# Sketched attention and a leaky MLP in one kernel: v on every fourth partition, the first batch's features turned by TensorE, alpha turned later, a new order

## The chip, the cores and the metric

The kernel runs on one NeuronCore of a Trainium2 chip. The metric is the device time of one execution in microseconds (us), the median of several runs, lower is better. The core has TensorE (PE, matrix products; its weight loads are listed as PEld), VectorE (DVE), ScalarE (ACT), GpSimd (POOL) and SyncE (SP), whose queue issues nearly all the DMA transfers here. Products accumulate in PSUM, a memory of 8 banks; everything else lies in SBUF, 128 partitions wide.

## The reference, cut to what matters

There are 4 batches, 4 heads, 1,088 tokens, a head width of 32 and two sketches S1 and S2 of 8 rows each. The feature of a vector is the outer product of its two sketches, 64 numbers:

```python
phi(x) = (S1 x) outer (S2 x)                    # [.., 64]
kv  = sum over tokens of phi(k) v               # [64, 32] per batch and head
z   = sum over tokens of phi(k)                 # [64]
x   = (phi(q) kv) / (phi(q) z + 1e-6)           # attention output, [4352, 128] over batch and token
h   = x @ w_in                                  # [4352, 2048]
out = (max(h, 0) + alpha * min(h, 0)) @ w_out   # [4352, 128]
```

The kernel writes the leaky part as relu(h) times (1 - alpha) w_out plus x times a folded matrix W = w_in diag(alpha) w_out. W is computed once on the chip from bf16 high and low parts of w_out.

## The kernel before, in words

The kernel is a list of operations, each with its engine or engines, a cost in ns, dependences, buffers and a due time. A planner (`plan`) walks this list with a model of each engine and fixes the order in which each engine gets its instructions. Due times are worked out backwards from the end and then moved by a table `SHIFT`, one entry per operation name. Each engine then works through its instructions in the planned order; the waits follow from the dependences. A DMA load costs the planner 60 ns on the queue that issues it, and the table `FIRST` says when its data are taken to arrive, wherever the load stands in the queue.

*Loads.* SP issues k of batch 0 in two pieces (k0.0, k0.1), the first part of q (q0.0), v of batch 0 in four transfers (v0), the rest of q (q0.1), then the weights in halves (w_in0, w_out0, w_in1, w_out1), then k1, q1, v1. Batches 2 and 3 are loaded after the first stores. ACT's queue issues the sketches (`rows`), a small rest of k and alpha (`arows`). A partition holds 34 tokens of one head, and each head has 32 partitions. v is held with 32 neighbouring partitions for each quarter of the slots.

*Keys (`key_part`, `keys`).* k is turned by DVE (L592) in blocks of 32 x 32. PE makes the sketches (L598, operations "ab"), 32 rows at a time; DVE turns them back token-major (L601, "abT"). DVE or POOL form the outer products kp (L614). PE sums z (L638, L644) and kv (L653, L658, "kv0.0", "kv0.1", "kv1.0" and so on); z goes through a mask and a product with S1sel (L667, L670, "zM") and is added up by DVE into the third part of Wq (L673, "zW"), with which q's features give the denominator. kv is copied (bs), turned by PE (L681, "fin") and copied into kvW.

*Queries (`query_part`).* q is turned by DVE (L693). PE computes the features, two sketches and the denominator's weights in one go, 32 rows at a time (L699, "f"); it needs zW. DVE turns them (L705, "fT0" and "fT1"), multiplies (L711, "denm"), sums and inverts (L716, L717), scales (L721, "rec") and forms the outer product (L732, "ph"), then turns that (L735, "phT"). PE multiplies with kvW (L746, "num"); ACT or DVE copy the result as xT in bf16. Batch 0 is done in two parts, q0.0 and q0.1.

*Weights.* w_in is cast to bf16 (L362 on ACT, L364 on DVE) and turned by PE (L564, "winT"); w_out gives three bf16 versions (w_a, w_hi, w_lo: L548, L539, L362, L364), and PE forms W (L573).

*MLP (`mlp`).* For each group of tokens and each of 16 chunks of 128 hidden units, PE computes h (L812), ACT or DVE the relu (L818, L820), and PE adds the second product (L833, L830 in the last group). The first of them is called h0.0. DVE turns the result (L840), and SP stores it (L852).

While PE waits early on, it runs dummy matmuls on constants (L480); the planner fills gaps with one dummy per `DUMMY` ns until `FILL`. A load is entered like this:

```python
o = op("sp" if eng == "sp" else "act", 60, emit, due=-1e6 + len(ops), name="ld " + name)
o.arrive = t
```

Of the kernel before, what the change touches and what calls it, by code (L numbers as in the profile page):

```python
# [11 lines left out]
F32 = mybir.dt.float32  # L12
# [22 lines left out]
class Op:  # L35
# [24 lines left out]
FILL, DUMMY = 20000, 220.0  # L60
# [5 lines left out]
    "S": -162063, "S1rep": -165092, "S1sel": -117129, "Sq": -118882, "W": -37412, "W0": -22866, "W1": 15478,  # L66
    "W2": -15123, "W3": 1781, "W4": 2619, "W5": 51587, "W6": 25967, "W7": 192714, "W8": 115002, "W9": 219619,
    "Wmm": -33330, "alpha": -190724, "alphaT": -266286, "fin0": -14043, "fin1": 12778, "fin2": 12779, "fin3": 56137,
    "h0.0": -78145, "h0.1": -75522, "h0.10": -65056, "h0.11": -64907, "h0.12": -60138, "h0.13": -56202,
    "h0.14": -54167, "h0.15": -52572, "h0.2": -74191, "h0.3": -73871, "h0.4": -73366, "h0.5": -73505, "h0.6": -74028,  # L70
    "h0.7": -71518, "h0.8": -69689, "h0.9": -65371, "h1.0": -34789, "h1.1": -34107, "h1.10": -26669, "h1.11": -25965,
    "h1.12": -24240, "h1.13": -23831, "h1.14": -22996, "h1.15": -21303, "h1.2": -32211, "h1.3": -30635,
    "h1.4": -29890, "h1.5": -29256, "h1.6": -28989, "h1.7": -28705, "h1.8": -27953, "h1.9": -28414, "h2.0": -22166,
    "h2.1": -20590, "h2.10": -18021, "h2.11": -17163, "h2.12": -16727, "h2.13": -16702, "h2.14": -12616,
    "h2.15": -11871, "h2.2": -21026, "h2.3": -21311, "h2.4": -19650, "h2.5": -19181, "h2.6": -18910, "h2.7": -19344,
    "h2.8": -17740, "h2.9": -18101, "h3.0": -3542, "h3.1": -3314, "h3.10": -5050, "h3.11": -4032, "h3.12": -4085,
    "h3.13": -3612, "h3.14": -3253, "h3.15": -185, "h3.2": -3701, "h3.3": -4173, "h3.4": -4620, "h3.5": -4847,
    "h3.6": -4746, "h3.7": -4882, "h3.8": -5316, "h3.9": -4570, "h4.0": 1358, "h4.1": 1685, "h4.10": 1468,
    "h4.11": 1195, "h4.12": 1628, "h4.13": 2054, "h4.14": 1887, "h4.15": 2269, "h4.2": 1790, "h4.3": 2027,
    "h4.4": 1529, "h4.5": 1001, "h4.6": 2156, "h4.7": 2376, "h4.8": 2356, "h4.9": 2026, "h5.0": 623, "h5.1": 112,  # L80
    "h5.10": 629, "h5.11": 320, "h5.12": 6246, "h5.13": 6167, "h5.14": 5978, "h5.15": 5769, "h5.2": 1403, "h5.3": 942,
    "h5.4": 617, "h5.5": 311, "h5.6": -87, "h5.7": 177, "h5.8": 596, "h5.9": 1190, "h6.0": 6190, "h6.1": 6591,
    "h6.10": 13032, "h6.11": 16054, "h6.12": 17584, "h6.13": 21801, "h6.14": 21493, "h6.15": 24820, "h6.2": 6396,
    "h6.3": 6161, "h6.4": 5844, "h6.5": 5396, "h6.6": 5964, "h6.7": 9398, "h6.8": 11454, "h6.9": 12503, "h7.0": 24810,
    "h7.1": 25740, "h7.10": 39860, "h7.11": 39788, "h7.12": 40696, "h7.13": 42107, "h7.14": 48471, "h7.15": 65935,
    "h7.2": 31811, "h7.3": 31675, "h7.4": 34383, "h7.5": 34600, "h7.6": 36091, "h7.7": 36311, "h7.8": 37161,
    "h7.9": 37561, "h8.0": 65178, "h8.1": 67716, "h8.10": 91782, "h8.11": 93060, "h8.12": 93208, "h8.13": 95018,
    "h8.14": 105798, "h8.15": 109119, "h8.2": 67942, "h8.3": 67800, "h8.4": 70787, "h8.5": 81498, "h8.6": 82124,
    "h8.7": 84958, "h8.8": 87782, "h8.9": 90633, "h9.0": 115646, "h9.1": 118850, "h9.10": 171489, "h9.11": 175089,
    "h9.12": 186470, "h9.13": 195972, "h9.14": 195962, "h9.15": 220234, "h9.2": 130914, "h9.3": 130993,  # L90
    "h9.4": 132808, "h9.5": 137804, "h9.6": 144756, "h9.7": 145191, "h9.8": 147495, "h9.9": 158749, "ident": -173975,
    "identb": -65399, "k0.0T": -269499, "k0.0ab": -208500, "k0.0abT": -181386, "k0.0kp0": -186006, "k0.0kp1": -49805,
    "k0.1T": -226397, "k0.1ab": -204602, "k0.1abT": -147845, "k0.1kp0": -80610, "k0.1kp1": -126124, "k1T": -151807,
    "k1ab": -65617, "k1abT": -64202, "k1kp0": -53416, "k1kp1": -50262, "k2T": -49013, "k2ab": -24485, "k2abT": -23171,
    "k2kp0": -4748, "k2kp1": -20747, "k3T": 1061, "k3ab": -476, "k3abT": 976, "k3kp0": -5300, "k3kp1": 4934,
    "kv0.0": -128612, "kv0.1": -38075, "kv1.0": -12328, "kv2.0": -3408, "kv3.0": 3898, "kvW0": -45486, "kvW1": 1981,
    "kvW2": 13506, "kvW3": 1305, "kvc0": -39856, "kvc1": 5618, "kvc2": -187, "kvc3": 21281, "mask4": -7204,
    "masks": -230084, "o0.0": -68831, "o0.1": -35165, "o0.10": -11755, "o0.11": -37900, "o0.12": -22687,
    "o0.13": -2667, "o0.14": -19472, "o0.15": -17633, "o0.2": -26624, "o0.3": -50154, "o0.4": -53802, "o0.5": -52091,
    "o0.6": 7406, "o0.7": -19776, "o0.8": -55070, "o0.9": -22190, "o1.0": -19212, "o1.1": -10753, "o1.10": -12412,  # L100
    "o1.11": -9725, "o1.12": 12884, "o1.13": 5281, "o1.14": 5421, "o1.15": 10070, "o1.2": 5939, "o1.3": -7592,
    "o1.4": -1373, "o1.5": 16588, "o1.6": 16406, "o1.7": -12906, "o1.8": -12480, "o1.9": -13846, "o2.0": -13883,
    "o2.1": 7536, "o2.10": -3705, "o2.11": 12909, "o2.12": 5832, "o2.13": 6569, "o2.14": 7440, "o2.15": -481,
    "o2.2": 11555, "o2.3": -6618, "o2.4": 8785, "o2.5": 3950, "o2.6": -13616, "o2.7": -8748, "o2.8": 1638,
    "o2.9": -2544, "o3.0": -2366, "o3.1": 14406, "o3.10": 2060, "o3.11": 30488, "o3.12": 1602, "o3.13": 38819,
    "o3.14": -177, "o3.15": 4596, "o3.2": 406, "o3.3": 5117, "o3.4": 3644, "o3.5": 10266, "o3.6": 5165, "o3.7": 1159,
    "o3.8": 27826, "o3.9": 571, "o4.0": 2412, "o4.1": 11935, "o4.10": 29557, "o4.11": 4726, "o4.12": 19429,
    "o4.13": 19816, "o4.14": 19315, "o4.15": 10373, "o4.2": 4269, "o4.3": 8227, "o4.4": 42796, "o4.5": 32283,
    "o4.6": 17095, "o4.7": 24031, "o4.8": 6192, "o4.9": 30133, "o5.0": 14462, "o5.1": 22177, "o5.10": 17762,
    "o5.11": 14812, "o5.12": 36034, "o5.13": 93554, "o5.14": 18463, "o5.15": 89195, "o5.2": 58370, "o5.3": 17242,  # L110
    "o5.4": 63152, "o5.5": 13846, "o5.6": 58588, "o5.7": 14941, "o5.8": 24115, "o5.9": 52316, "o6.0": 24146,
    "o6.1": 55471, "o6.10": 45589, "o6.11": 53978, "o6.12": 28311, "o6.13": 24237, "o6.14": 36282, "o6.15": 26859,
    "o6.2": 108485, "o6.3": 118186, "o6.4": 118170, "o6.5": 24511, "o6.6": 76818, "o6.7": 185418, "o6.8": 65222,
    "o6.9": 53201, "o7.0": 53882, "o7.1": 159116, "o7.10": 70280, "o7.11": 85883, "o7.12": 81416, "o7.13": 219320,
    "o7.14": 125582, "o7.15": 145328, "o7.2": 220110, "o7.3": 219471, "o7.4": 87638, "o7.5": 86532, "o7.6": 271772,
    "o7.7": 97668, "o7.8": 52125, "o7.9": 218098, "o8.0": 95600, "o8.1": 100801, "o8.10": 188787, "o8.11": 126719,
    "o8.12": 191640, "o8.13": 206438, "o8.14": 130480, "o8.15": 139549, "o8.2": 114097, "o8.3": 159936,
    "o8.4": 194146, "o8.5": 132532, "o8.6": 188660, "o8.7": 119852, "o8.8": 118698, "o8.9": 126302, "o9.0": 155601,
    "o9.1": 265875, "o9.10": 251564, "o9.11": 247170, "o9.12": 207643, "o9.13": 239424, "o9.14": 211858,
    "o9.15": 265764, "o9.2": 198072, "o9.3": 216795, "o9.4": 176212, "o9.5": 162237, "o9.6": 188998, "o9.7": 188709,  # L120
    "o9.8": 220317, "o9.9": 255881, "oT0": -76595, "oT1": -13249, "oT2": -4976, "oT3": 3666, "oT4": 8797, "oT5": 9428,
    "oT6": 59626, "oT7": 86089, "oT8": 150669, "oT9.0": 181249, "oT9.1": 157151, "q0.0T": -206015, "q0.0den": -23594,
    "q0.0denm": -84715, "q0.0f": -154699, "q0.0fT0": -154405, "q0.0fT1": -84045, "q0.0num": -84185,
    "q0.0ph0": -127812, "q0.0phT0": -84287, "q0.0rec": -2266, "q0.0x0.0": -30236, "q0.0x0.1": -80540,
    "q0.1T": -127197, "q0.1den": -70835, "q0.1denm": -74338, "q0.1f": -127426, "q0.1fT0": -75331, "q0.1fT1": -93816,
    "q0.1num": -26548, "q0.1ph0": -45509, "q0.1phT0": -34568, "q0.1rec": -27567, "q0.1x1.0": -19689,
    "q0.1x1.1": -14970, "q1T": -78399, "q1den": -20535, "q1denm": -28588, "q1f": -27994, "q1fT0": 2661,
# [797 lines left out]
```

## Time and profile before

| what | value |
|---|---|
| median of 3 runs | 109.66 us (108.98 to 109.77) |
| profiled execution | 110.35 us, span 108.6 us |
| PE busy | 100.8 us (93%), 1,368 instructions |
| PEld, DVE, ACT, POOL busy | 51.7, 77.9, 69.7, 38.0 us |
| mean granted TensorE clock | 0.98 |
| DMA | 26,255 packets, 11.24 MB, mean 104 GB/s |

The span goes from the first to the last instruction on the core; the execution's own time is a little longer. The slices of the page are 40 equal parts of the span, each digit the busy share in tenths. PEclk is the granted TensorE clock in tenths of full speed. The chain of waits goes back from the last instruction: at each step to what released it, or to the instruction before it on its engine; each line there has a start, a length and what ran. In the table by stretches of time, the columns after the stretch are its length, busy us and number of instructions of PE, PEld, DVE, ACT and POOL, the granted clock, the share of 16 DMA engines and GB/s.

### The profile page before, as it was taken

How to read it: one execution, taken by the hardware profiler on the slowest of the kernel's cores; microseconds unless marked ns; L12 is line 12 of the kernel's file. 1: busy time of each engine (PE TensorE's matmuls, PEld its weight loads, DVE VectorE, ACT ScalarE, POOL GpSimd, SP SyncE). 2: the span in 40 equal slices, each digit the busy share in tenths (PEclk: the TensorE clock that was granted, in tenths of full speed). 3: DMA queues.
4: the chain of work that ended last, by engine and by line, in shares of the span. 5: the costliest groups of instructions: out<-in, count | busy, mean ns of one | idle time of the engine just before them, and what ended most of it. 6: DMA issues, size and time to landing. Idle time of an engine off the chain costs nothing.

```text
span 108.6 us, 3312 instructions
## 1 busy us (share of the span) xinstructions
PE 100.8 (93%) x1368; PEld 51.7 (48%) x1368; DVE 77.9 (72%) x139; ACT 69.7 (64%) x152; POOL 38.0 (35%) x28
## 2 busy tenths in 40 slices
PE   7949997999999999999999999999999999999930
PEld 2233454443556543533455444355444445788920
DVE  3256399999678899388399995895982677577710
ACT  0510534999622699299685976677895688788920
POOL 4007383059994650001946504908700000000000
PEclk9996799999999999999999999999999999999998
DMA  2999999700000037995990500050032023051221
GB/s 58 320 213 259 340 356 313 140 24 6 0 0 9 0 57 139 378 182 96 359 221 14 89 8 6 0 97 6 0 59 38 0 49 54 2 95 27 48 46 36
DMA packets 26255, 11.24 MB, mean 104 GB/s; under 512 B 17776, under 2 KB 25216, under 8 KB 26240
## 3 DMA queue, kind: packets, MB, share of 16 engines
q1 hardware_dynamic: 25840, 10.92, 40.9%
q8 instruction: 11, 0.18, 0.7%
q10 hardware_dynamic: 400, 0.11, 0.5%
q14 instruction: 4, 0.03, 0.1%
HBM read 8.80 MB, written 2.23 MB: 102 GB/s over the span
## 4 chain that ended last, share of the span: by engine, by line
PE 82%; DVE 7%; DMA 4%; ACTq 1%; issue 1%; ACT 0%
PE ps L812 28%; PE ps L833 28%; PE ps L746 5%; DMA arows<-in_moe_alpha_dram 4%; PE ps L480 4%; PE ps L653 3%; PE ps L573 2%; PE ps L699 2%; PE ps L598 2%; PE ps L830 2%; DVE ft__73 L705 1%; DVE tm__79 L711 1%; PE ps L638 1%; ACTq L384 1%; DVE pt__77 L735 1%; DVE ph__75 L732 1%
## 5 line engine op out<-in xcount | busy, mean ns | idle before, releaser
L812 PEld LDWEIGHTS <-w_in_bf 128*128 128x128 bf16 x160 | 15.2, 99 | 14.5 <-issue 2.3
L833 PEld LDWEIGHTS <-w 128*128 128x128 bf16 x144 | 13.7, 98 | 13.3 <-issue 2.2
L812 PE MATMUL ps<-xT__94,w_in_bf 128*128 128x512 bf16 (+1 forms) x80 | 20.0, 336 | 0.0
L812 PE MATMUL ps<-xT__93,w_in_bf 128*128 128x512 bf16 x64 | 19.3, 380 | 0.1
L818 ACT ACTIVATE rh__81<-ps 128x512 bf16<-128x512 f32 (+1 forms) x25 | 13.9, 556 | 4.9 <-PE ps L812 4.8
L614 POOL TENSOR_TENSOR kp__68<-ab__66 128x1152 f32<-128x1152 f32 (+1 forms) x4 | 8.1, 2022 | 24.0 <-DVE ab__66 L601 24.0
L480 PE MATMUL ps<-const-bfloat16-1.0 128*128 128x512 bf16 x33 | 12.2, 506 | 0.8 <-PEq L909 0.8
L818 ACT ACTIVATE rh__83<-ps 128x512 bf16<-128x512 f32 (+1 forms) x19 | 10.6, 557 | 1.5 <-PE ps L812 1.5
L818 ACT ACTIVATE rh__82<-ps 128x512 bf16<-128x512 f32 (+1 forms) x18 | 10.0, 555 | 1.3 <-PE ps L812 1.2
L732 POOL TENSOR_TENSOR ph__76<-ft__73 128x1024 f32<-128x1024 f32 (+1 forms) x3 | 8.6, 2856 | 4.8 <-DVE ft__73 L721 4.8
L818 ACT ACTIVATE rh__85<-ps 128x512 bf16<-128x512 f32 (+1 forms) x15 | 8.4, 562 | 2.0 <-PE ps L812 1.7
L833 PE MATMUL ps<-rh__81,w 128*128 128x512 bf16 (+1 forms) x24 | 8.6, 357 | 0.0
L818 ACT ACTIVATE rh__86<-ps 128x512 bf16<-128x512 f32 (+1 forms) x12 | 6.9, 571 | 2.6 <-PE ps L833 2.3
L833 PE MATMUL ps<-rh__82,w 128*128 128x512 bf16 (+1 forms) x21 | 7.6, 360 | 0.0
L746 PE MATMUL ps<-pt__77,kvW 32*32 32x288 f32 (+3 forms) x320 | 7.4, 353 | 0.1
L735 DVE STREAM_TRANSPOSE pt__77<-ph__75 128x1280 f32<-128x1280 f32 (+1 forms) x5 | 6.9, 1388 | 0.7 <-POOL ph__75 L732 0.7
L539 POOL TENSOR_TENSOR w<-w_out_f,w 128x512 bf16<-128x512 f32 x4 | 4.7, 1165 | 7.6 <-DVE w L364 5.5
L705 DVE STREAM_TRANSPOSE ft__73<-ps 128x576 f32<-128x576 f32 (+2 forms) x10 | 6.0, 638 | 1.7 <-PE ps L699 1.5
L614 POOL TENSOR_TENSOR kp__69<-ab__66 128x1152 f32<-128x1152 f32 x3 | 6.5, 2176 | 0.0
L833 PE MATMUL ps<-rh__83,w 128*128 128x512 bf16 (+1 forms) x18 | 6.5, 361 | 0.0
L833 PE MATMUL ps<-rh__84,w 128*128 128x512 bf16 (+1 forms) x18 | 6.4, 355 | 0.0
L833 PE MATMUL ps<-rh__85,w 128*128 128x512 bf16 (+1 forms) x18 | 6.4, 355 | 0.0
(144 smaller groups left out, 193.7 us busy)
## 6 DMA issues: line engine op xcount, KB each, us to landing
k<-in_k_dram SPq DMA_DIRECT2D x3, 544.0 KB, 4.2
q<-in_q_dram SPq DMA_DIRECT2D x3, 544.0 KB, 7.8
out_dram<-oT__89 SPq DMA_DIRECT2D x24, 64.0 KB, 1.9
v<-in_v_dram SPq DMA_DIRECT2D x9, 128.0 KB, 7.0
w_in_f<-in_moe_w_in_dram SPq DMA_DIRECT2D x2, 512.0 KB, 6.3
w_out_f<-in_moe_w_out_dram SPq DMA_DIRECT2D x2, 512.0 KB, 6.4
v<-in_v_dram SPq DMA_DIRECT2D x6, 144.0 KB, 7.5
k<-in_k_dram SPq DMA_DIRECT2D x2, 256.0 KB, 3.8
```

What stands on the lines that cost most here:

```text
L480: nc.tensor.matmul(PS[:, 7], ones(128), ones(512), start=True, stop=True, skip_group_check=True)
L539: return lambda e: (nc.vector if e == "dve" else nc.gpsimd).tensor_tensor(out=out, in0=a, in1=b, op=what)
L573: nc.tensor.matmul(ps(bw)[:, :3 * DM], winT[:, c], w3[:, c].rearrange("p y m -> p (y m)"), start=c == 0, stop=c == NC - 1)
L614: (nc.vector if e == "dve" else nc.gpsimd).tensor_tensor(out=dst, in0=i0, in1=i1, op=ALU.mult)
L653: nc.tensor.matmul(ps(bk)[32 * h:32 * h + 32, :R], v_sb[b][:, h, vs], at(sb(bkp[h // 2]), x, [[1, R]]), start=first and i == 0, stop=False ...
L705: nc.vector.transpose(at(sb(bf)[:, 0], 2 * y * D, [[D, 2], [H * D, ns], [1, D]]), ps(f2[y])[:, :, :n].rearrange("p h (s t) -> p h s t", t=D))
L732: (nc.vector if e == "dve" else nc.gpsimd).tensor_tensor(out=dst, in0=i0, in1=i1, op=ALU.mult)
L735: oT.append(op("dve", dv(k) + 35, lambda e, lo=lo, hi=hi, bph=bph: nc.vector.transpose(sb(bp)[:, lo:hi].rearrange("p a b -> p (a b)"), sb( ...
L746: nc.tensor.matmul(ps(n2[c // 2])[32 * h:32 * h + 32, c % 2, :w * D], kvW[b][P, y, h], at(sb(bp)[P, 0], (2 * h + y) * D, [[2 * H * D, w], ...
L812: nc.tensor.matmul(ps(b)[:, :n], w_in_bf[:, c * 128:(c + 1) * 128], xs(), start=True, stop=True)
L818: nc.scalar.activation(sb(br)[:, :n], ps(b)[:, :n], ACTF.Relu)
L833: nc.tensor.matmul(ps(bo)[:, :n], w, y(), start=c == 0, stop=c == NC)
```

## The change

- **v on every fourth partition.** Token slots are now dealt out so that quarter c of the slots lies on partitions c, c+4, c+8 and so on, 9 slots for the first three quarters and 7 for the last, padded with zeros by a DVE memset ("pads") on which all v loads now depend. k is turned into the same order by two DVE instructions, with zeros set by POOL ("pads2"). The remainders of z and kv over 32 or 64 rows go away.
- **Batch 0's features token-major from PE.** The weights of these products are 128 tokens of turned k or q, and the moving side is the small sketch matrix. The results come out token-major, so that a copy on ACT or DVE stands where DVE turned them. For q, the denominator's part is a product of its own ("w", from Ww0), 8 or 10 products each, and denm reads it from PSUM.
- **Alpha turned later.** Its turn on PE now depends on the product that replicates the sketches (S1rep). The rest of k is no longer on ACT's queue.
- **Order planned anew.** The planner's costs, `FIRST` and `SHIFT` are new (the entry of "pads" is 19620207), `DUMMY` is 320, w_in's cast and w_hi may run on POOL, denm and rec too, and the memset "zero" counts 1,700 ns.

The order that the planner now gives SP is k0.0, k0.1, q0.0, w_in0, w_out0, q0.1, w_in1, w_out1, k1, q1, v0, v1, and after them the first store. PE gets 7 dummies, the turn of the sketches, S1rep, the turn of alpha, k0.0ab, a dummy, k0.1ab, z0.0, a dummy, z0.1, q0.0f, zM0, kv0.0, q0.0w, kv0.1, winT0, fin0, 4 dummies, q0.1f, a dummy, q0.1w, num0.0, winT1 and then h0.0. DVE gets, after denm, sums, reciprocal and scaling of q0.0: w_a, the copy of winT0, the turn of q0.1, phT of q0.0. POOL gets ph of q0.0; both copies of the first x are ACT's. In the new file the line of h is L881, of kv L699, of batch 0's query products L748, of the outer product ph L802.

```diff
-FILL, DUMMY = 20000, 220.0
+FILL, DUMMY = 20000, 320.0
...
+    for o in reversed(ops):
+        for d in [] if o.late else o.deps:
+            d.due = min(d.due, o.due)
     waiting = sorted(ops, key=lambda o: o.due)
...
+    def pads(e):
+        for x in v_sb:
+            nc.vector.memset(x[:, :, 7:9], 0.0)
+
+    def pads2(e):
+        nc.gpsimd.memset(kZ[1], 0.0)
+        for x in tiles["kT"]:
+            nc.gpsimd.memset(x, 0.0)
+
+    c_pad = op("dve", 1, pads, due=-2e7, name="pads")
...
     def load_v(b):
         for c in range(4):
+            n = 9 if c < 3 else 7
+            load(f"v{b}", "sp", v_sb[b][c:128:4, :, :n].rearrange("p h s d -> p h (s d)"),
+                 bass.AP(tensor=v.tensor, offset=(b * H * S + 9 * c) * D, ap=[[NT * D, 32], [S * D, H], [1, n * D]]),
+                 32 * H * n * D * 4).deps.append(c_pad)
...
-    load_k0("k0.0", 0)
-    load_k0("k0.1", 1)
+    load_k0("k0.0", 0, 4)
+    load_k0("k0.1", 4, 5)
     load_rows("q0.0", q_sb, q, 0, 0, 16)
-    load_v0()
-    load_rows("q0.1", q_sb, q, 0, 16, NT)
+    load_v(0)
     load_w_in(0)
     load_w_out(0)
+    load_rows("q0.1", q_sb, q, 0, 16, NT)
...
-    op("dve", 1150, zeros, due=-1e7, name="zero")
+    op("dve", 1700, zeros, due=-1e7, name="zero")
...
     o = op("pe", 180, lambda e: nc.tensor.transpose(ps(b_al)[:, :NC], arows, ident[:NC, :NC]),
-           [c_id] + got("arows"), [b_al], 200, name="alphaT", mode=1, ni=2)
+           [c_id, c_rep] + got("arows"), [b_al], 200, name="alphaT", mode=1, ni=2)
...
+        def turned(e):
+            for s in range(ns):
+                for hp in range(2):
+                    P = slice(64 * hp, 64 * hp + 64)
+                    nc.tensor.matmul(ps(pair)[:, hp, s * D:s * D + D], kT()[P, 4 * D * s:4 * D * s + 4 * D],
+                                     Wk[P].rearrange("p a b c -> p (a b c)"), start=True, stop=True, skip_group_check=True)
...
+            def kv(e, bkp=bkp, base=base, ns=ns, lo=lo, first=first, last=last):
+                for s in range(ns):
                     for h in range(H):
                         x = (base[h // 2] + 2 * s + h % 2) * R
+                        nc.tensor.matmul(ps(bk)[32 * h:32 * h + 32, :R], v_sb[b][:, h, lo + s], at(sb(bkp[h // 2]), x, [[1, R]]),
+                                         start=first and s == 0, stop=last and s == ns - 1, skip_group_check=True)
...
+            def rows_of(w, wide, dst):
+                def f(e):
+                    for s in range(ns):
+                        for hp in range(2):
+                            P = slice(64 * hp, 64 * hp + 64)
+                            x = 4 * D * s if s < 4 else (nj - 4) * D
+                            nc.tensor.matmul(ps(dst)[:, hp, s * wide:s * wide + wide], sb(bT)[P, x:x + 4 * D], w(P), start=True, stop=True,
+                                             skip_group_check=True)
+                return f
...
+            ot.append(op("pe", 100 * ns + 60, rows_of(lambda P: Ww0[P], 2 * r, bw), [oq, w_done[b]], [bT, bw], 200,
+                         name=tag + "w", mode=1, ni=8 * ns))
...
+                nc.vector.tensor_mul(at(sb(bt)[:, 0], 0, [[24 * ns, 2], [12, 2 * ns], [1, r]]), at(sb(bf)[:, 0], r, [[2 * ns * D, 2], [D, 2 * ns], [1, r]]),
+                                     at(ps(bw), 0, [[512, 2], [r, 2 * ns], [1, r]]))
```

## The prediction

> **What bounds the kernel now.** I read the page's slices first: they show when TensorE (PE) is full.
>
> ```profile
> PE   7949997999999999999999999999999999999930
> PEclk9996799999999999999999999999999999999998
> DMA  2999999700000037995990500050032023051221
> ```
>
> A slice is 2.7 us. From the ninth (about 22 us) until near the end PE is at 9; before that it partly waits and runs dummy matmuls (L480), and the DMA engines are at 9 from the second slice into the seventh. So the time is a front until the first MLP matmul, a body that PE bounds, and a tail. The chain of waits, in order of time, gives the borders.
>
> ```profile
> 12.51 0.58 PE ps L653 x32
> ...
> 13.87 0.56 PE ps L699 x32
> ...
> 14.45 0.79 DVE ft__73 L705 x2
> ...
> 18.80 1.25 DVE pt__77 L735
> ...
> 21.80 0.37 DVE xT__93 L364
> ...
> 22.22 1.47 PE ps L812 x6
> ```
>
> The first L812 starts at 22.22, 8.35 us after q0.0's features (L699 at 13.87). The last L830 ends at 104.04. Front 22.2, body 81.8 (PE busy 81.8 in the stretches from 22.2 to 104.1: nothing to win there but PE work), tail 4.6: span 108.6. The profiled execution took 110.35, 1.75 beyond its span and 0.69 over the median of 109.66. I add the difference to both.
>
> Next, stretches of time: the two last columns are the DMA share and GB/s.
>
> ```profile
> 0.00:6.00 6.00, 4.42 (x10) 1.31 (x10) 1.74 (x8) 1.49 (x2) 1.22 (x8) 1.00 0.71 189
> 6.00:12.00 6.00, 5.18 (x53) 1.97 (x53) 3.30 (x7) 0.74 (x3) 3.03 (x2) 0.73 1.02 258
> 12.00:18.00 6.00, 5.45 (x145) 3.28 (x145) 5.25 (x12) 2.08 (x5) 3.31 (x3) 0.99 1.10 362
> 18.00:22.00 4.00, 3.89 (x114) 1.97 (x111) 3.86 (x8) 3.78 (x10) 0.00 (x0) 1.00 0.81 144
> ```
>
> The DMA engines are full from 2 to 18 us: what stands behind in SP's queue lands late. The weights show it. Issued at 6.40, 6.88, 7.50 and 9.95, they landed (issue plus time to landing) at 11.6, 13.3, 15.0 and 16.4: in order of issue, 1.6 us apart for 512 KB.
>
> **The change part by part.** The step that decides is a moved DMA. SP issued v0 fourth, behind k0's two pieces and q0.0, and kv0.0 (L653) ran at 12.51. Now SP issues k0, q0.0, w_in0, w_out0, q0.1, w_in1, w_out1, k1, q1 and only then v0: the v loads depend on the memset "pads", which the planner puts behind 1,700 ns of "zero" on DVE, and the loads without that dependence take its SP slots of 60 ns before. On PE the order is z0.0, z0.1, q0.0f, zM0, kv0.0, q0.0w, kv0.1, winT0, fin0, q0.1f, q0.1w, num0.0, winT1, h0.0. kv0.0 waits for v0, and q0.0w, on which the whole first x hangs, is queued behind it.
>
> *When v0 lands.* Bytes up to its end: k0, q0, v0, k1, q1 of 544 KB each and 2,048 KB of weights, 4,768 KB or 4.88 MB. The stretches move 6 x (0.189 + 0.258 + 0.362) = 4.85 MB by 18.0, so 18.1. The other way: w_out1 landed at 16.4 with v0 ahead of it; without v0 (0.557 MB at some 270 GB/s, 2.1) 14.3; k1 and q1 at the 387 GB/s of 16 to 18 us take 2.9, v0 at that rate 1.4: 18.6. I take 18.4. Lower end 17.0, if v0 and the early pieces go at the best rate; upper end 22.5, where q1 landed (issued 13.33, 9.2 to landing) with as many bytes ahead of its end as v0 now has.
>
> The row for v itself: 18 to 20 us, mostly v1, moved 204 GB/s, against 387 from 16 to 18, mostly k1 and q1. [...]
>
> *From v0 to the first MLP matmul.* All earlier work on k0 and q0.0 is long done. Steps:
> - kv0.0, 32 passes: 0.58 at full clock, up to 1.2 at half; 0.8.
> - q0.0w: 8 fp32 products of 2 passes with 128 weight columns. Not in the trace: below, L699's 0.56 for 32 narrow passes gives 0.3; above, L670's 0.34 for 2 passes gives 2.7; nearest, 8 transposes with 128 columns (L564) in 0.61, 0.076 each; 1.2.
> - denm: 0.33 alone, 1.08 behind a POOL operation (L711 has both); 0.45. Sum, reciprocal, scaling: 0.32 + 0.26 + 0.27.
> - ph, 1,024 elements, on POOL where DVE took 1.24: 2.60 (L732's row), up to 0.7 more behind DVE's w_a, as kp__68 on POOL took 1.56 beside a DVE product of 0.69. Then phT 1.25.
> - So phT could end 8.0 after v0. But PE runs in order: q0.1f and q0.1w (20 passes, 1.5 each by L564) stand ahead of num0.0, and q0.1f waits for DVE's w_a 0.7, winT copy 0.68 and the turn of q0.1 0.86. That lets num0.0 start at 8.9, or at 7.7 with cheaper passes. num 1.3, two copies on ACT 0.37 each (before, one ran on DVE), steps 0.15.
> Sum 9.8 to 11.1; I take 10.3, ends 9.0 and 11.5. The first MLP matmul stands at 18.4 + 10.3 = 28.7, which is 6.5 later.
>
> *What is gained.* The transposes fT (0.79) go, and the stall of denm (0.7); their places are in the sum above. On batches 1 to 3 kv loses its 32- and 64-row remainder: 1.03 + 0.25 becomes 36/32 x 1.03 = 1.16, and z about 0.1: 0.6 in all of PE work. Against it stand the start of the body, where ACT and DVE still carry w_a, w_lo and a winT copy when the first relus come due (0 to 1.2): 0.6. Body unchanged. The wait covers all the rest: the memsets (POOL 2,944 elements, 2.4 by 0.20 for 128 and 0.10 for 1), alpha turned after the sketches instead of before them (PE waited for it until 6.82), twice-issued key transposes, fewer dummies. If v0 came early, alpha would be next: its turn still stands ahead of k0.0's features.
>
> Total: 110.35 + 6.5 = 116.85 for the profiled execution, **116.2** against the median.
>
> **The rivals.** *A late tail* (0.10): v0 ends where q1 ended, 22.5; +10.6, 120.3. For it speaks that the DMA row dribbles from 18 to 24 us; against it, that the weights landed without such a tail.
>
> *A cold restart* (0.15). After 1.6 us without work PE ran at 0.73 on average from 6 to 12 us, full again after 12.2; that is 3.4 us at half. Now PE has some 8 us with nothing to do, and a further gap before num0.0. If the body starts at half clock, 16 matmuls take 3.4 instead of 1.7: 117.9. Against it, PE works most of the 10 us behind v0. [...]
>
> *v0 does not hold* (0.05, the other side: faster). If v0's packets pass the queued ones, so that it lands before about 11 us, kv0.0 waits for kp alone and q0.0w runs at 12.0: 12.0 + 1.2 + 0.45 + 0.85 + 2.9 + 1.25 + 1.3 + 0.95 = 20.9, 1.3 earlier, and 0.6 of PE work is saved: 107.8. The point is where v0's landing plus 0.8 equals 12. For it: v0's transfers are small. Against it: the weights landed in the order of issue.
>
> *v0 by half* (0.03 same; 0.05 slower by 1 to 3%): landing at 13 to 16, so 110 to 112.5.
>
> **How the numbers follow.** The forecast has 0.62, from 17.0 + 9.0 = 26.0 (+3.8, less the 0.6 of PE work: 112.9) to about 118. Beside it late tail 0.10, cold 0.15, half 0.08, not holding 0.05. The range 112.5 to 120.0 leaves out 0.05 + 0.03 + 0.05 below and some 0.06 of the tail above. A measurement of this kernel tells about 1% from nothing. Slower by over 1%: 0.62 + 0.10 + 0.15 + 0.05 = 0.92; within 0.03; faster 0.05.
>
> **What would show it.** In the profile after: kv0.0's first matmul starts at 18 to 20 with a wait of some 8 us for v's DMA; the PE row has three or more low slices between 10 and 18 us; the first L881 (h0.0) starts near 28.7; from there to the last PE work 81 to 83 us; ph on POOL 2.6 or more. The step is wrong if v0 lands before 16 or if q0.0w runs ahead of it; the size is wrong if num0.0 starts earlier than 7 us behind v0's landing.

## The result, and the profile after

The changed kernel takes 120.15 us (median of 4 runs, 119.0 to 121.04) against 109.51 us for the kernel before on the same chip (4 runs, 108.98 to 109.77). The ratio is 1.089, with a 95% interval of 1.081 to 1.098; it leaves out executions over 1.5% above the fastest of their kernel, here the two of 120.84 and 121.04 us, the first of which is the profiled one. The ratio stands for 119.3 us, inside the predicted range; the median of all four lies just above the range's end of 120.0. The predicted 116.2 us had the sign and the place, and it is 3 us short by the ratio, 4 by the median.

The profiled execution took 120.84 us, its span is 119.1. Of the 10.5 us that the span has grown, 9.05 lie ahead of the first MLP matmul (31.27 instead of 22.22), 2.24 between it and the end of PE's work (31.27 to 115.32, 84.05 us; before 81.81), and the tail is 0.8 shorter (3.8 instead of 4.6). The last of PE's work in the changed kernel:

```profile
115.05 0.27 PE L899 MATMUL ps<-W_bf,xT__94 128*128 128x128 bf16 x2
```

The slices of the changed kernel, 3 us each:

```profile
PE   7999405999999999959999989999999999999970
PEclk9999999999599999999999999999999999999998
DMA  3999995000000002694279322000002205026222
```

PE is at 4 and 0 in the fifth and sixth slice, 12 to 18 us, and the DMA engines are full until the end of the sixth. PE falls to 5 once more in the eighteenth. The waits of PE, with the total, the number and the longest:

```profile
PE ps L699 <- DMA v<-in_v_dram: 5.8, 1, 5.8
PE ps L881 <- DVE rh__84 L889: 1.2, 1, 1.2
```

The first is kv0.0 waiting for v0 (the prediction had some 8 us for it), the second an MLP matmul waiting for a relu that comes late in batch 1. The chain of waits around the front's end (start, length, what ran):

```profile
14.51 4.53 DMA v<-in_v_dram
...
19.08 1.08 PE ps L699 x32
20.16 1.82 PE ps L748 x16
21.99 1.22 PE ps L699 x40
23.21 0.97 PE ps L582 x8
24.18 0.43 PE ps L722 x2
24.61 1.69 PE ps L494 x4
26.30 1.24 PE ps L748 x20
...
27.86 1.22 PE ps L748 x20
29.08 1.23 PE ps L816 x61
30.30 0.97 PE ps L582 x8
31.27 2.42 PE ps L881 x7
```

In the code's names: v0 lands, then kv0.0, q0.0w, kv0.1, winT0, fin0, four dummies, q0.1f, a dummy, q0.1w, num0.0, winT1, h0.0. From v0 to h0.0 PE has no gap to speak of, yet it needs 12.2 us. q0.0w's 16 passes take 1.82 us, q0.1f's 20 passes 1.24: the first run at about twice the time for a pass. The clock row reads full there and can't be taken at its word: this trace has no record of the clock before 26.1 us, and the row counts such time as full. In later runs the 16 passes of q0.0w took 1.82 at a granted clock of 0.50 and 1.00 at 1.00. So the durations say half clock until the dummies, full for q0.1f to q0.1w, and half again for winT1 and the first MLP matmuls: seven took 2.42 us, where a later run at full clock has 1.67. From 26.1 us on the record agrees: 1.00 from 26.1 to 29.5, 0.50 from 29.6 to 33.0, 1.00 from 33.0 to 36.4.

The late relu, in the timeline of DVE and POOL (start, length, engine, line):

```profile
47.22 2.39 POOL L802 TENSOR_TENSOR ph__76<-ft__73 128x1280 f32<-128x1280 f32 x1 [1.67 <-DVE ft__73 L791]
...
47.65 3.03 DVE L802 TENSOR_TENSOR ph__75<-ft__73 128x1024 f32<-128x1024 f32 x1
...
51.89 0.65 DVE L889 TENSOR_SCALAR rh__84<-ps 128x512 bf16<-128x512 f32 x1
```

DVE's outer product (1.24 when alone) ended 1.07 after POOL's, and the turn and the relu queued behind it followed late.

### The profile page after: what moved, and what is told of

The parts are those of the page before. It is cut to its first block, busy times and chain, and to the rows that moved or that the text cites. A ratio compares the mean times of both kernels' runs of the same rounds, so it can differ in the third digit from the quotient of the medians.

```text
span 119.1 us, 3344 instructions
## 1 busy us (share of the span) xinstructions
PE 106.9 (90%) x1353; PEld 61.3 (52%) x1353; DVE 78.3 (66%) x137; ACT 71.5 (60%) x166; POOL 40.0 (34%) x32
## 4 chain that ended last, share of the span: by engine, by line
PE 70%; DVE 10%; DMA 9%; SPq 5%; issue 3%
PE ps L902 20%; PE ps L881 19%; DMA v<-in_v_dram 8%; PE ps L494 5%; PE ps L816 5%; SPq L388 4%; PE ps L699 4%; PE ps L748 4%; PE ps L637 3%; DVE ph__75 L802 2%; PE ps L591 2%; DVE kT__64 L629 2%; PE ps L582 2%; SPq L921 2%; PE ps L770 1%
## 5 line engine op out<-in xcount | busy, mean ns | idle before, releaser
L881 PEld LDWEIGHTS <-w_in_bf 128*128 128x128 bf16 x160 | 15.5, 100 | 15.1 <-issue 3.9
L881 PE MATMUL ps<-xT__93,w_in_bf 128*128 128x512 bf16 x64 | 19.3, 396 | 1.2 <-DVE rh__84 L889 1.2
L881 PE MATMUL ps<-xT__94,w_in_bf 128*128 128x512 bf16 (+1 forms) x80 | 18.6, 336 | 0.0
L887 ACT ACTIVATE rh__81<-ps 128x512 bf16<-128x512 f32 (+1 forms) x24 | 13.9, 578 | 4.5 <-PE ps L881 2.4
L802 POOL TENSOR_TENSOR ph__75<-ft__73 128x1024 f32<-128x1024 f32 (+1 forms) x4 | 8.5, 2137 | 22.2 <-DVE ft__73 L791 22.2
L887 ACT ACTIVATE rh__83<-ps 128x512 bf16<-128x512 f32 (+1 forms) x18 | 9.9, 553 | 2.0 <-PE ps L881 1.7
L887 ACT ACTIVATE rh__82<-ps 128x512 bf16<-128x512 f32 (+1 forms) x18 | 9.9, 553 | 1.4 <-PE ps L902 0.7
L699 PE MATMUL ps<-kp__68,v 128*32 128x64 f32 x140 | 4.7, 242 | 5.8 <-DMA v<-in_v_dram 5.8
L366 ACT COPY bs__99<-ps 128x256 f32<-128x256 f32 x4 | 1.5, 372 | 13.3 <-PE ps L699 11.2
L902 PE MATMUL ps<-rh__81,w 128*128 128x512 bf16 (+1 forms) x25 | 9.0, 361 | 0.0
L887 ACT ACTIVATE rh__87<-ps 128x512 bf16<-128x512 f32 (+1 forms) x14 | 7.2, 516 | 2.4 <-PE ps L881 2.3
L887 ACT ACTIVATE rh__84<-ps 128x512 bf16<-128x512 f32 (+1 forms) x14 | 8.0, 569 | 0.2 <-PE ps L902 0.2
L902 PE MATMUL ps<-rh__82,w 128*128 128x512 bf16 (+1 forms) x22 | 7.9, 360 | 0.0
L802 POOL TENSOR_TENSOR ph__76<-ft__73 128x1280 f32<-128x1280 f32 x3 | 7.2, 2388 | 1.7 <-DVE ft__73 L791 1.7
L902 PE MATMUL ps<-rh__83,w 128*128 128x512 bf16 (+1 forms) x21 | 7.5, 359 | 0.0
L494 PE MATMUL ps<-const-bfloat16-1.0 128*128 128x512 bf16 x14 | 6.7, 607 | 0.8 <-PEq L978 0.8
L887 ACT ACTIVATE rh__85<-ps 128x512 bf16<-128x512 f32 (+1 forms) x13 | 7.2, 552 | 0.3 <-PE ps L902 0.3
L762 DVE TENSOR_TENSOR tm__79<-ft__73,ps 128x128 f32<-128x128 f32 (+1 forms) x2 | 0.6, 303 | 10.0 <-PE ps L748 7.9
L699 PEld LDWEIGHTS ps<-kp__68,v 128*32 128x32 f32 x140 | 4.0, 123 | 6.2 <-DMA v<-in_v_dram 6.0
```

The lines of the kernel that those rows point to most:

```text
L494: nc.tensor.matmul(PS[:, 7], ones(128), ones(512), start=True, stop=True, skip_group_check=True)
L699: nc.tensor.matmul(ps(bk)[32 * h:32 * h + 32, :R], v_sb[b][:, h, lo + s], at(sb(bkp[h // 2]), x, [[1, R]]), start=first and s == 0, stop=l ...
L802: (nc.vector if e == "dve" else nc.gpsimd).tensor_tensor(out=dst, in0=i0, in1=i1, op=ALU.mult)
L881: nc.tensor.matmul(ps(b)[:, :n], w_in_bf[:, c * 128:(c + 1) * 128], xs(), start=True, stop=True)
L887: nc.scalar.activation(sb(br)[:, :n], ps(b)[:, :n], ACTF.Relu)
L902: nc.tensor.matmul(ps(bo)[:, :n], w, y(), start=c == 0, stop=c == NC)
```

## The experiments

**v0 early, everything else as changed.** One entry of the table goes, so that "pads" runs first and SP issues v0 fourth:

```diff
-    "pads": 19620207, "pads2": 12570,
+    "pads2": 12570,
```

> The changed kernel with one entry of its order removed: the memset "pads" comes first on VectorE again, so that SP issues v0 fourth, behind k0 and q0.0, as in the kernel before. All other instructions keep their order on every engine. Theory (the late v0 is the cause): v0 lands before 11 us, kv0.0 runs at about 12.6 without a wait on v, the first MLP matmul (L881) starts at 22 to 24.5 instead of 31.3, and the time is 109.5 to 112. Rival (the slowdown sits in something else, in the features by products or in the later turn of alpha): the first MLP matmul stays at 28 or later, and the time stays at 117 to 121.

Measured: 113.03 us (112.73 to 114.82), ratio to before 1.039 (1.027 to 1.050). The chain of waits of this kernel:

```profile
11.37 1.01 PE ps L699 x32
12.38 1.82 PE ps L748 x16
...
21.07 1.23 PE ps L816 x63
22.30 0.96 PE ps L582 x8
23.27 2.31 PE ps L881 x7
```

kv0.0 runs at 11.4 without a wait and h0.0 starts at 23.3, 8.0 us earlier. The ratio falls from 1.089 to 1.039, which is 5.5 us (6.7 when this kernel was run again, below): the place of v0 carries more than half of the loss. But 113 is above what I had expected at most (112), and above before. The other 3 to 4 us are in the rest of the change. The table by stretches shows where to look (length, PE busy and instructions, granted clock, DMA share, GB/s):

```profile
8.00:12.00 4.00, 4.00 (x67) 0.50 0.83 225
12.00:16.00 4.00, 4.00 (x79) 0.50 1.03 302
16.00:18.00 2.00, 2.00 (x10) 0.52 1.07 195
18.00:21.50 3.50, 3.50 (x81) 0.98 0.89 334
21.50:25.00 3.50, 3.50 (x50) 0.54 0.20 71
```

PE is busy without a break, and its granted clock is at half for ten microseconds.

**The kernel before with v0 late, nothing else.**

```diff
-    load_v0()
     load_rows("q0.1", q_sb, q, 0, 16, NT)
...
         load_rows(f"q{b}", q_sb, q, b)
+        if b == 1:
+            load_v0()
         load_v(b)
```

> The kernel before with one step moved: the loads of v0 are issued on SP behind q1 (ahead of v1), nothing else. Theory: the place in the queue alone makes the loss. v0, here on 32 neighbouring partitions, lands at 19 to 22, kv0.0 waits for it, the first MLP matmul stands some 8 to 10 us behind it at 28 to 31, and the time is 116 to 120. Rival (the place is harmless without the rest of the change, since v's packets pass the queued ones or PE has other work): v0 lands before 14, and the time is within 1.5 us of before.

Measured: 120.39 us (119.33 to 122.12), ratio 1.104 (1.088 to 1.121). Its chain:

```profile
13.50 8.27 DMA v<-in_v_dram
...
21.97 1.08 PE ps L654 x32
...
33.41 1.47 PE ps L813 x6
```

The place in the queue alone makes a loss as large as the changed kernel's. The time is a little above the 116 to 120 expected. v0 lands at 21.8 and the first MLP matmul follows 11.6 us later, longer than the 8 to 10 expected. From there to the end of PE's work it is 81.8 us, as before. With v0 late, the rest of the change is thus worth nothing on balance: v0 lands 2.7 us earlier, the stretch behind it is 0.6 longer, the body 2.2 longer, and the tail is the same 3.8. This kernel's tail is written as before's, and so is that of the run without dummies below, which has 3.8 as well; so the 4.6 belongs to the profiled execution of before, and the 0.8 is no gain of the change.

**PE kept at work through the wait.** In the changed kernel:

```diff
     for o in plan(ops, classes):
+        if o.name == "kv0.0":
+            o.fill += 26
         dummy(o.fill)
```

> The changed kernel with 26 more dummy matmuls (bfloat16, 512 columns) on TensorE ahead of kv0.0, so that PE works through the wait for v0. Theory (the 12.2 us from v0 to the first MLP matmul, where 10.3 were predicted, come from half clock behind the wait): kv0.0 takes 0.6 to 0.8 instead of 1.08, q0.0w 1.0 to 1.3 instead of 1.82, the first seven MLP matmuls 1.5 instead of 2.42, and the time is 2 to 3.5 us below the changed kernel's: 116 to 118. Rival (VectorE and GpSimd set that stretch): the same 12.2, and the time within 1 us of the changed kernel's.

Measured: 118.45 us (117.48 to 120.39), ratio 1.087 (1.069 to 1.104), which overlaps the changed kernel's. By the ratios the gain is 0.3 us, not the 2 to 3.5 expected, and not certain; the times alone do not settle the theory. The chain does:

```profile
13.38 7.14 PE ps L494 x26
20.53 0.58 PE ps L699 x32
21.11 1.02 PE ps L748 x16
...
29.91 1.67 PE ps L881 x7
```

kv0.0 took 0.58 instead of 1.08, q0.0w 1.02 instead of 1.82, the first seven MLP matmuls 1.67 instead of 2.42, all as the theory had it. From kv0.0 to h0.0 it is 9.4 us instead of 12.2. Of these 2.8 the dummies themselves took back half, since kv0.0 started 1.45 later, behind the last of them; h0.0 starts 1.36 earlier. The body is 0.65 shorter (29.91 to 113.31), the tail 0.2 longer, and the span 1.8 shorter. These are differences between two single executions. That half clock lengthens the stretch is shown; that dummies in the wait make the kernel faster is not.

**Early v0, and batch 1's product on GpSimd.**

```diff
     for o in plan(ops, classes):
+        if o.name == "q1ph0":
+            o.on = "pool"
```

> The kernel of the early v0 (the changed kernel with "pads" first), and batch 1's first feature product (q1ph0, 1,024 elements) on GpSimd instead of VectorE, where it took 3.03 us beside GpSimd's 1,280 elements of 2.39; emission order as it was. Theory (two products that run at the same time on VectorE and GpSimd hold each other up, and the relu behind them then stalls PE by 1.2 us): the product takes 1.9 to 2.3 on GpSimd, the stall before the out product of rh__84 goes, and the time is 0.8 to 1.3 us below the early v0's alone. Rival (the stall was of the late body's making and is not there with the early v0, or the second product now comes late): within 0.5 us of the early v0's, or above it.

Measured: 113.33 us (111.58 to 114.51), ratio 1.046 (1.030 to 1.062). In the trace the wait for rh__84 is gone, the product takes 1.95 us on GpSimd, but the spread of the runs hides what that is worth. In the profiles both bodies begin at half clock (seven MLP matmuls in 2.31 and 2.41 us), and the body is 82.7 instead of 84.0. Both were run once more:

> The kernel of the early v0 once more, beside the next one on the same chip: 112.5 to 113.5.

> The kernel of the early v0 with q1ph0 on GpSimd once more, since its median and the early v0's lay within their spread while its trace had lost the stall of 1.2 us. Theory (the stall is worth its 1.2 us): 0.8 to 1.3 us below the kernel above. Rival (another delay takes its place): within 0.4 us of it.

Measured: 112.29 us for the early v0 (111.75 to 114.62; ratio 1.028, 1.021 to 1.034), a little below the 112.5 to 113.5 expected, and 111.74 with the product on GpSimd (111.42 to 115.81; 1.024, 1.018 to 1.029). The difference in the ratios is 0.4 us and not certain. The body is 0.6 us shorter in the trace (82.8 instead of 83.4). The stall's 1.2 is gone from it, but in the second kernel's profile the first seven MLP matmuls took 2.48 us instead of 1.67, which gives 0.8 back. It need not come from the edit: in the stretch from 21.5 to 25 us the granted clock was 1.00 in this execution of the early v0 (the line below), 0.54 in the earlier one of the same kernel, shown above.

```profile
21.50:25.00 3.50, 3.35 (x60) 1.00 0.00 0
```

**More dummies in the front, and an earlier turn of q0.1.** Three kernels on top of the last (early v0, product on GpSimd): 25 more dummies spread over the front; the same with the turn of q0.1 moved ahead of denm and two dummies ahead of q0.1f; the turn alone, without the four dummies that fill the wait for it. The cut shows the first two together:

```diff
+    todo = plan(ops, classes)
+    turn = next(o for o in todo if o.name == "q0.1T")
+    todo.remove(turn)
+    todo.insert(next(i for i, o in enumerate(todo) if o.name == "q0.0denm"), turn)
+    WARM = {"k0.1ab": 1, "z0.0": 2, "q0.0f": 3, "zM0": 2, "kv0.0": 3, "q0.0w": 3, "kv0.1": 4, "winT0": 2, "q0.1w": 3, "q0.0num": 2}
...
+        o.fill += WARM.get(o.name, 0)
```

> The kernel of the early v0 with q1ph0 on GpSimd, and 25 more dummy matmuls on TensorE spread over its front (1 to 4 ahead of each of ten operations between k0.1ab and q0.0num). In the kernel of the early v0 the granted clock is half from 8 to 18 us although PE is never idle there, and q0.0f and q0.0w take 1.85 and 1.83 us for 16 passes, where the late v0 behind 26 dummies had 1.02. Theory (the narrow fp32 products do not count as work for the clock, so that the front and the first MLP matmuls run at half clock): with the dummies q0.0w takes 1.0 to 1.2, the first seven MLP matmuls 1.5 to 1.7 instead of 2.4; 25 dummies of 0.22 cost 5.4 us, less what lies in waits of PE, so the first MLP matmul stands at 21 to 24 and the time is 0 to 2 us below the early v0's with q1ph0 on GpSimd. Rival (the products are bound by their weight loads or by another engine, not by the clock): they stay at 1.8, the front grows by 4 to 5 us, and so does the time.

> The same with the turn of q0.1 (L609, L612 on VectorE) moved ahead of q0.0's denm, into a gap of VectorE of 2 us, and 2 instead of 4 dummies ahead of q0.1f. Theory: in the kernel of the early v0 num0.0 is ready at 19.2 (phT's end) but runs at 21.1, because q0.1f, ahead of it on PE, waits behind dummies until 18.3 for the turn of q0.1 (16.95 to 17.77 on VectorE). With the turn early and the clock full, num0.0 waits for phT alone, the first MLP matmul stands at 19.5 to 22, and the time is 1.5 to 3 us below that of the dummies alone. Rival (the later weights, their casts on ScalarE, or k1 and q1, which land at 19 to 20, bound the body next): the front is as much shorter, but PE stalls behind it and the time is the same.

> The kernel of the early v0 with q1ph0 on GpSimd, the turn of q0.1 moved ahead of q0.0's denm as above, no dummies ahead of q0.1f, and none added. Theory (the clock decides): the four dummies that went were what brought the clock to full at 18.2, so q0.1f and q0.1w take 2.2 to 2.4 each at half clock instead of 1.24, num0.0 starts at 20.5 to 21.5 in spite of the earlier turn, and the time is within 1 us of the early v0's with q1ph0 on GpSimd. Rival (the order alone decides): q0.1f runs at 16.8, num0.0 at 19.2 to 19.5, and the time falls by 1.5 to 2 us.

Measured: 116.93 us (113.65 to 118.01) with the dummies, 117.16 (112.95 to 118.22) with dummies and turn. Three of the four executions of each took 116.2 to 118.2, the profiled ones among them; the fourth took 113.65 and 112.95 and has no profile. In the profiles the mechanism is there and the sum was wrong. The chain of the first:

```profile
8.56 0.97 PE ps L494 x2
...
15.12 1.28 PE ps L494 x3
...
18.18 1.00 PE ps L748 x16
...
28.99 1.67 PE ps L881 x7
```

At full clock q0.0w takes 1.00 and the first MLP matmuls 1.67, as expected. But a dummy issued at half clock costs 0.43 to 0.49 us, not 0.22, and so few in a place brought the clock back only at about 17.4 us in the first (0.50 from 12 to 16, 0.65 from 16 to 18, then 1.00). The first MLP matmul stood at 29.0 and 29.9, not at 19.5 to 24. In these executions, where PE has no idle time in the front, the dummies cost more than they returned; what they cost in the shorter ones is not known. Whether the earlier turn helps at full clock is left open, for num0.0 was held up by the dummies.

The turn alone: 113.68 us (112.09 to 114.97), ratio 1.034 (1.024 to 1.044). Its chain:

```profile
17.30 2.28 PE ps L748 x20
...
20.11 2.25 PE ps L748 x20
22.37 1.45 PE ps L816 x64
...
24.78 2.99 PE ps L881 x7
```

q0.1f ran a microsecond earlier, and took 2.28 instead of 1.24. That is what the clock theory gave, within the 2.2 to 2.4 written down; num0.0 is even later than its range (22.4 against 20.5 to 21.5). The rival, that the order alone decides, would have had num0.0 at 19.2 to 19.5. The four dummies that looked like filling had been what brought the clock back: from 18 to 21.5 us it was 0.50 here, 0.98 and 1.00 in the two profiles of the early v0, and 0.95 in the second one with the product on GpSimd.

**The kernel before without its dummies in the front.**

```diff
-        dummy(o.fill)
+        dummy(0)
```

> The kernel before without the dummy matmuls that its plan puts into the waits of PE in the front (the seven at the start stay). Theory (the dummies keep the clock, and the narrow fp32 products by themselves do not): the granted clock stays at half through the front, L653's 32 passes take 1.0 instead of 0.58, the first MLP matmul starts 0.3 to 1.5 us later and the body's first matmuls run at half clock; 1 to 3 us slower than before. Rival (the front of before hangs on VectorE alone and the clock comes up by itself): within 0.5 us of before.

Measured: 110.18 us (109.48 to 110.82), ratio 1.0065 (1.0027 to 1.0103): 0.7 us, less than the theory's 1 to 3 and more than the rival's 0.5 at the median, though its interval covers part of both. Stretch and chain:

```profile
8.00:12.00 4.00, 2.92 (x70) 0.50 1.10 298
12.00:16.00 4.00, 2.65 (x82) 0.50 1.14 360
```

```profile
22.11 2.37 PE ps L812 x6
```

The clock was at half through the front, as the theory has it, and the first six MLP matmuls took 2.37 instead of 1.47 us. But they start at 22.11, where before had 22.22. The front of before hangs on VectorE (without the dummies on ScalarE's casts and copies too), and slower products vanish in PE's waits. So half clock costs the kernel before 0.9 us at the body's start and next to nothing in the front; in the changed kernel, whose front is made of PE's own products, it costs the front too.

**v's partitions.** Two runs on what the pattern is worth, with loads that nothing uses. In the kernel before, while the DMA engines are idle:

```diff
+        if o.name in ("h0.4", "h0.12"):
+            nc.vector.memset(spare[:, 0, 0, 0:1], 0.0)
+            for c in range(4):
+                m = 9 if c < 3 else 7
+                dst = spare[32 * c:32 * c + 32] if o.name == "h0.4" else spare[c:128:4]
+                nc.sync.dma_start(dst[:, :, :m].rearrange("p h s d -> p h (s d)"),
+                                  bass.AP(tensor=v.tensor, offset=9 * c * D, ap=[[NT * D, 32], [S * D, H], [1, m * D]]))
```

> The kernel before with one addition that nothing uses: while the DMA engines have nothing else to do, batch 0's v is loaded twice more into a spare tile, by four pieces each on SP, first with 32 neighbouring partitions to a piece (released by a memset emitted behind h0.4), then with every fourth partition (behind h0.12). Bytes and descriptors in DRAM are the same. Theory (the partitions of a piece set its rate): the packets of the first take 80 ns and more, those of the second 45 to 65; from the first packet to the last the second is shorter, by up to 1.3 us. Rival (the landing of v0 was earlier in the changed kernel only because of what else was in the queue): packets and landings alike within 10%. The time is not compared.

The queue's totals, from 25.5 to 29.5 us (neighbours) and from 31 to 34.5 us (every fourth), with packets, MB and the share of 16 engines' time:

```profile
q1 hardware_dynamic: 576, 0.56, 52.5%
...
q1 hardware_dynamic: 576, 0.56, 59.3%
```

In the mean over all packets, the 64 small ones included, one took 0.525 x 16 x 4.0 us / 576 = 58 ns in the first and 0.593 x 16 x 3.5 / 576 = 58 in the second. In idle engines the patterns are equal; the theory failed there. So the neighbours were put in the very place of the late v0:

```diff
+    spared = []
     for o in plan(ops, classes):
+        if o.name == "ld v0" and not spared:
+            spared.append(1)
+            for c in range(4):
+                nc.sync.dma_start(at(k_sb[3][32 * c:32 * c + 32], 0, [[8 * D, H], [1, 8 * D]]),
+                                  bass.AP(tensor=v.tensor, offset=8 * c * D, ap=[[NT * D, 32], [S * D, H], [1, 8 * D]]))
```

> The changed kernel with four more loads of batch 0's v on SP in the very place of its late v0 (behind q1): 32 neighbouring partitions and 128 KB to a piece, into a tile that is not read before its own load (k of batch 3). The late v0 on every fourth partition follows behind them. In the idle DMA engines the two patterns were alike (packets of 1,152 bytes 65 and 70 ns); this compares them while k1 and q1 are still on their way, against the changed kernel, where the pieces of v0 took 3.0 us and more to land, with the last at about 19. Theory (neighbouring partitions are slow only beside other transfers): their packets take 80 ns and more, and the last of the four pieces lands 1.0 us or more later than v0 did, at 20 to 21. Rival (the pattern makes no difference here either): packets of 45 to 65 ns, and the last piece lands at 18.2 to 19.2. The time is not compared; v0 now lands some 2 us later by its own bytes.

From 16 to 18 us (length, granted clock, DMA share, GB/s), with the neighbours:

```profile
16.00:18.00 2.00, 0.50 1.10 217
```

and in the changed kernel:

```profile
16.00:18.00 2.00, 1.00 1.03 334
```

With engines as full, the stretch with the neighbours moved 217 GB/s, the one with every fourth partition 334; the ends of q1 are in both. The next 2 us of the run with the neighbours, mostly v0 on every fourth partition, moved 263 at a DMA share of 1.03. The first three of the four pieces were issued at 10.85, 11.35 and 11.82 and took 7.4, 7.5 and 7.5 us to land: 18.3, 18.8 and 19.3. The fourth has no landing in the trace; by the same step it is at 19.8, an estimate. The changed kernel's v0 came down at 18.0, 18.3, 18.7 and 19.04. That is 0.3 to 0.8 later, with pieces of 128 KB instead of 144; q1 too landed later, at 18.0 instead of 17.6. It is neither the theory's 1.0 nor the rival's nothing. Beside other transfers the neighbours were slower (217 against 334 GB/s), alone they were not (58 ns a packet both ways); why is not settled.

## Why the prediction was right or wrong

**The step that decides was right.** v0 behind q1 makes the larger part of the loss: undone, the first MLP matmul comes 8.0 us earlier, and by the ratios 5.5 to 6.7 us of 9.8 come back; done alone, the kernel before loses 11. PE's order held it up as described: kv0.0 waits, and q0.0w stands behind it.

**v0's landing** was 0.6 late: 19.04 against 18.4, inside its 17.0 to 22.5. The forecast has v0 at the 387 GB/s of 16 to 18 us, 1.4 us; at the 204 of 18 to 20 it would have been 2.7, and the landing 1.3 later. No run shows that every fourth partition gets 387: the changed kernel moved 334 GB/s from 16 to 18 us and 211 from 18 to 20. What the runs show is a difference between the patterns under load, 217 against 334 GB/s, and none with idle engines, 58 ns a packet both ways. Of the 1.3 us the run with the neighbours has 0.3 to 0.8. Between the two kernels with a late v0 the landings are 2.7 apart (21.8 and 19.04), but there q1 was issued 0.55 later as well, so the size stays open.

**From v0 to the first MLP matmul** is the term that was mis-sized: 12.2 against 10.3, above the upper end of 11.5. What I had taken for the other engines held. phT ended 8.0 us behind v0, as worked out; ph took 2.26 on POOL, a little under 2.60; from num0.0 to h0.0 it was 2.2. Wrong was PE's own row: num0.0 started 10.0 behind v0, where I had 7.7 to 8.9. I had priced kv0.0 and q0.0w somewhere between full and half clock and left kv0.1, winT0, fin0 and the dummies ahead of q0.1f unpriced, as if they lay beside other work. They stand in PE's order in front of num0.0, at half clock. PE's row, added up: 1.08 + 1.82 + 1.22 + 0.97 + 0.43 + 1.69 + 1.24 + 0.32 + 1.22 = 9.99, of which the unpriced ones (kv0.1, winT0, fin0, four dummies) are 4.3. The run with PE kept at work has num0.0 at 7.7 behind kv0.0 (28.20 against 20.53): the 7.7 was the price at full clock. The same step fails in the sum for "v0 does not hold": it gave 20.9 for the first MLP matmul, and with the early v0 it stands at 22.8 and 23.3.

**The body** was said to be unchanged and is 2.24 longer. The start at half clock costs some 0.7 (2.42 against 1.67 for the first seven matmuls; the whole body is 0.65 shorter with PE kept at work). It was my rival "a cold restart", which had 1.7 for it (3.4 us at half clock, which is eight matmuls of 0.22 at full clock, not the sixteen it names), but I let it act on the body alone and not on the stretch before, and set it beside the forecast instead of in it. "PE works most of the 10 us behind v0" was the argument against it, and that argument failed: PE did work, and up to the dummies its durations stayed those of half clock (1.82 us for q0.0w, 1.02 with PE kept at work). The stall of 1.2 behind the two outer products was not foreseen; the profile before has a case of it, the two L732 products at 36.2, of which POOL's took 3.25. Without these two the body is 82.1, 0.3 longer than before; where the 0.6 saved in z and kv and the 0.6 lost at its start went is not shown.

**The rivals.** A late tail: no, v0 landed at 19. v0 not holding, by half: no. Taken together, 0.6 of landing, 1.9 behind it and 2.2 of body, less 0.8 in the tail, make the 4.0 between the predicted and the measured profiled execution (116.85 and 120.84). The 0.8 is luck: it is not of the change, and it makes the miss look smaller. Had I added the cold restart to both places at what it measured, the centre would have stood near 119 (116.2, and 1.9 and 0.7).

**What neither the diff nor the sum showed** is that the rest of the change is a loss by itself: with v0 early it is 2.8 to 3.9% slower than before. The first MLP matmul stands 0.6 and 1.1 us later than before, and the body is 1.6 and 2.2 longer, of which the stall is 1.2. For the front the durations suggest the reason: features from PE take DVE's turns out of it and put fp32 products of 16 and 32 columns in; PE then has no waits for dummies, and runs the front at half clock (0.50 from 8 to 16 us with v0 early). In the kernel before, the clock from 12 to 16 us was 0.98 with the dummies in its waits and 0.50 without. No run has that front at full clock without added work, so its share is argued and not shown. None of the kernels tried beats before.

## What to carry to other kernels

Price the operations behind a wait at the clock that they will get, and price all of them that stand ahead in the engine's order, the fillers too: here q0.0w took 1.82 us and not 1.02, and the unpriced ones made 4.3. The wait was paid twice in this kernel, once as the wait (5.8 us) and once in the work behind it (12.2 us instead of the 9.4 with PE kept at work). That the wait alone brought half clock is not shown: q0.0f, ahead of it, had run its 16 passes in 1.92 us as well. Keeping PE at work has a price too, and here returned 0.3 us by the ratios. Before a dependence is added to a load, look at what the queue issues in the meantime: one small memset put late cost this kernel 5.5 to 6.7 us.

## What the runs showed of the hardware that was not expected

- **Busy, and still at half clock.** With v0 early, PE was busy 4.00 us of 4.00 from 8 to 12 and again from 12 to 16, most of it with narrow fp32 products, and the granted clock was 0.50 in both. Behind the turns of w_in and four dummies of 512 columns in bf16 it was 0.98 in the stretch from 18 to 21.5; without the four dummies it was 0.50. In the changed kernel half clock came back once more behind full clock: 1.00 in the 3.4 us before 29.5, 0.50 from 29.6 to 33.0, 1.00 in the 3.4 us after, with PE busy all through. So busy by the profile did not by itself mean full clock here; what sets it is not shown.
- **The same kernel, another clock.** In two executions of the early v0, the stretch from 21.5 to 25 us had 0.54 and 1.00, and the first seven MLP matmuls took 2.31 and 1.67 us. What set it in either execution no run here shows.
- **An fp32 pass with 128 weight columns** (L748) costs 0.062 us at full clock (20 in 1.24) and 0.114 at half (16 in 1.82, 20 in 2.28), for 16 as for 32 moving columns (20 in 1.22 and 1.24): eight products of two passes make 1.0 to 1.8, where I had bounds of 0.3 and 2.7.
- **Two outer products at once on DVE and POOL** ended one after the other: DVE's took 3.03 us, ending 1.07 after POOL's, where it takes 1.24 alone. In the kernel before POOL's took 3.25 in such a pair, where the same 1,024 elements took 1.95 without it.
